# Retention with a mixture of attention experts: value products from the last key blocks, one write of v, a y table of one chunk, more buffers and a new order of the work

## The chip, the core and the metric

The kernel runs on one core of a Trainium2 chip. The core has a matrix engine (TensorE, PE in the profile; its weight loads are PEld), a vector engine (DVE), a scalar engine (ACT), GpSimd (POOL), and a queue engine (SP) that issues nearly all transfers here. Each takes its instructions in a fixed order. Matrix products land in PSUM, eight banks of 512 float32 columns on 128 partitions. The metric is the time of one execution in microseconds (us).

## The reference

Two stages follow each other. The first is retention: for 4 batches and 8 heads a 64x64 state runs over 768 positions.

```python
for t in range(S):
    state = gamma[None, :, None, None] * state + np.einsum('bhd,bhe->bhde', k[:, :, t], v[:, :, t])
    y[:, :, t] = scale * np.einsum('bhd,bhde->bhe', q[:, :, t], state)
```

Its output, laid side by side for the heads, is the x (4 x 768 x 512) of the second stage: four attention experts with one head of 64 each, of which every position uses the two with the highest gate logits.

```python
logits = x @ w_gate                      # top 2 of 4 experts, softmax weights w over the two
for e in range(E):
    q = x @ wq[e]; k = x @ wk[e]; v = x @ wv[e]
    scores = scale * (q @ k.transpose(0, 2, 1))
    scores = np.where(causal, -1000000000.0, scores)
    a = softmax(scores)
    out += (weight of e where it was chosen) * (a @ v @ wo[e])
```

Everything is float32.

## The kernel before, in words

The sequence is cut into 24 chunks g of 128 positions (six to a batch) and into 8 units j of 384 positions (two to a batch, so the odd unit of a batch attends to twice as many keys as the even one).

**Retention.** A chunk's q and k come in one load (`qkT_t`, three buffers), its k and v in natural order in another (`kv_t`, two buffers); `kdecay` scales the latter with powers of gamma. `h1(m)`, for half a chunk, adds to the state in PSUM (`ps_st`) and forms the part of y that comes from the state so far (`sblk`); `h2` forms the products inside the chunk, for which the scores are masked into one buffer (`am`). Then the DVE scales y out of PSUM by a table (`ys`, L307; the table `yt` holds 768 positions and is loaded in six pieces of 256 KB), ACT makes its rounded half `xh` (L309) and POOL the remainder `xl` (L311). All matrix products of the second stage are made of such halves.

**Experts.** `vgate(j, i)` forms v and the gate logits of a chunk, `proj` the q and k of two experts at a time. v stands with positions on partitions, and the value products need it with 32 keys on partitions: so v (in `vt`, a buffer of the four `pr`) goes to DRAM (`vd`) and comes back from there in four pieces (`vx`). It is written by two transfers, one for two experts each:

```python
def keep():
    for c in range(2):
        dma(vd.t[c].rearrange("i q n -> q i n"), vt.t[:, c * CH * 128:(c + 1) * CH * 128])
```

`pair(j, m)`, for 64 query positions and all four experts: scores into two banks (one or two spans of at most 512 keys), minimum on the DVE (L553, L558; scores have the sign turned), exponential with its sum on ACT (L565, into `pr`), the factor of sum and gate weight (L584 to L592), the scaling on POOL (L598) and a transposition in 32x32 blocks on the DVE (L605, into `pta` or `ptb`). There are six pairs to a unit, m = 0 to 5, with 64 more keys each. `av(j, k0, k1)` multiplies blocks of 32 keys with v and adds them up in four banks; an even unit has 12 key blocks, an odd one 24, in groups of six. The first matmul of a bank's sum starts it afresh (`start=k == 0`), and since all columns have to be started there, the groups run from the first key block on, which needs all six pairs. Then ACT and DVE take the two halves of the result (`oh` L650, `ol` L655, two buffers each), `wout(j, i)` multiplies with wo, ACT copies the result into `ot` (two buffers, shared with y) and SP stores it.

**The order.** The functions record operations; what is emitted is the list of numbers ORDER, one order over all engines, and SLOTS says which buffer each operation takes. In it the stages of three units overlap. An engine's instructions stand in the order of that list and wait for what they read and for their buffers to come free. At the start stand twelve products of a zeroed tile (`warm`) that write nothing of use.

## Time and profile before

| what | us |
|---|---|
| three runs | 323.5, 325.57, 328.87; median 325.57 |
| the profiled execution | 326.64 |
| its span, from the first to the last instruction | 324.7 |
| PE busy in it | 293.5 |
| DVE, ACT, POOL busy | 182.6, 152.2, 155.0 |

An engine is counted as busy while one of its instructions runs. A row of the timeline gives the start and duration of a run of equal instructions, and in brackets how long the engine had been idle and who ended that. In the chain of waits each piece is either work or a transfer that the next piece waited for. [...]

### The profile page before, as it was taken

To read this page: it belongs to the slowest core of one execution; us is meant where nothing else is said; L and a number is where in the kernel's file an instruction comes from. 1 tells how busy PE (TensorE), PEld (TensorE's weight loads), DVE (VectorE), ACT (ScalarE), POOL (GpSimd) and SP (SyncE) were. 2 spreads that over 40 slices of the span, in tenths; PEclk is the share of its full clock that TensorE was granted. 3 is DMA by queue.
4 is the path that set the end of the run, shared out by engine and by line. 5 is a ranking of instruction groups with operands and counts; after the bars stand their busy time and mean duration, and the time that the engine had idled before them with its cause. 6 is when DMAs were issued, how large, how long until landed. Compare 5 with 4: busy or idle time off the path is not lost.

```text
span 324.7 us, 14996 instructions
## 1 busy us (share of the span) xinstructions
PE 293.5 (90%) x6530; PEld 237.9 (73%) x6530; DVE 182.6 (56%) x567; ACT 152.2 (47%) x495; POOL 155.0 (48%) x281
## 2 busy tenths in 40 slices
PE   3879999979889999798999999999869999899695
PEld 1569979957579877676888987687668987527484
DVE  0242346586855676564676665667347544698601
ACT  2225355454454564445474452756426344366302
POOL 0257463855576362453729437166093623347300
PEclk9979999999979999999999999999989999999999
DMA  7898755752583345438447603343740013403103
GB/s 224 291 353 277 274 155 173 237 129 91 149 173 99 121 129 161 144 98 211 133 159 231 167 15 114 88 158 117 225 115 4 2 45 98 135 0 126 65 6 129
DMA packets 17106, 45.64 MB, mean 141 GB/s; under 512 B 2576, under 2 KB 5392, under 8 KB 17040
## 3 DMA queue, kind: packets, MB, share of 16 engines
q1 hardware_dynamic: 16896, 44.55, 44.2%
q8 instruction: 51, 0.84, 1.1%
q10 hardware_dynamic: 144, 0.13, 0.1%
q14 instruction: 15, 0.12, 0.1%
HBM read 35.23 MB, written 9.44 MB: 138 GB/s over the span
## 4 chain that ended last, share of the span: by engine, by line
PE 66%; DMA 10%; DVE 7%; POOL 6%; issue 5%; ACT 3%; SPq 1%; POOLq 0%; ACTq 0%; DVEq 0%
PE ps L130 61%; PE ps_st L130 5%; POOL pr L598 4%; DMA vd<-pr 4%; DMA out_dram<-ot 3%; ACT pr L565 2%; DVE ptb L605 2%; DVE ps L558 1%; DMA kv_t<-in_kv_dram 1%; ACT ot L686 1%; DMA kdec_t<-in_kdec_dram 1%; DMA vx<-vd 1%; SPq L133 1%; POOL kv_t L232 1%; DVE pta L605 1%
## 5 line engine op out<-in xcount | busy, mean ns | idle before, releaser
L598 POOL TENSOR_SCALAR pr<-pr,fs,wq 128x512 f32<-128x512 f32 (+7 forms) x128 | 77.0, 610 | 45.8 <-DVE fs L587 32.2
L565 ACT ACTIVATE pr<-ps,mn 128x512 f32<-128x512 f32 (+7 forms) x128 | 66.2, 521 | 58.8 <-DVE mn L558 25.1
L130 PE MATMUL ps<-kt,qt 64*64 64x512 f32 (+7 forms) x512 | 49.7, 439 | 0.6 <-ACT pr L565 0.4
L130 PE MATMUL ps<-xh,qk_hi 128*128 128x384 f32 x128 | 45.3, 354 | 2.6 <-ACT pr L565 2.6
L130 PE MATMUL ps<-xh,qk_lo 128*128 128x384 f32 x128 | 43.6, 340 | 2.5 <-issue 2.5
L605 DVE STREAM_TRANSPOSE ptb<-pr 128x448 f32<-128x448 f32 (+5 forms) x48 | 38.0, 800 | 11.4 <-POOL pr L598 11.4
L130 PE MATMUL ps<-xl,qk_hi 128*128 128x384 f32 x128 | 43.5, 340 | 0.0
L130 PE MATMUL ps_st<-kv_t 64*64 64x64 f32 x704 | 31.1, 226 | 9.9 <-DVE kv_t L232 5.4
L130 PEld LDWEIGHTS ps_st<-kv_t 64*64 64x64 f32 x704 | 27.4, 139 | 16.7 <-issue 5.9
L558 DVE CUSTOM_DVE_ANT_0 ps<-ps,mask 128x64 f32<-128x64 f32 (+7 forms) x64 | 28.1, 463 | 16.9 <-PE ps L130 16.6
L311 POOL TENSOR_TENSOR xl<-ot,xh 128x512 fp32r<-128x512 f32 x24 | 30.9, 1285 | 11.8 <-ACT xh L309 11.0
L130 PEld LDWEIGHTS ps<-ptb,vx 32*64 32x64 f32 x1504 | 27.4, 130 | 11.8 <-issue 8.4
L130 PE MATMUL ps<-ptb,vx 32*64 32x192 f32 (+5 forms) x1504 | 31.7, 296 | 4.5 <-issue 2.7
L232 POOL TENSOR_TENSOR kv_t<-kv_t,kdec_t 128x512 f32<-128x512 f32 x23 | 24.3, 1060 | 15.8 <-DMA kv_t<-in_kv_dram 12.1
L130 PEld LDWEIGHTS ps<-xh,qk_hi 128*128 128x128 f32 x128 | 24.2, 189 | 10.1 <-ACT pr L565 4.3
L130 PE MATMUL ps<-qkT_t 64*64 64x64 f32 x768 | 29.1, 223 | 2.1 <-ACT mn L575 1.4
L291 ACT ACTIVATE sblk<-ps_st 128x256 f32<-128x256 f32 x44 | 16.9, 383 | 29.9 <-PE ps_st L130 23.7
L130 PE MATMUL ps<-qkT_t,sblk 64*64 64x64 f32 x704 | 30.2, 223 | 0.6 <-issue 0.6
L130 PE MATMUL ps<-am,kv_t 64*64 64x64 f32 x768 | 28.7, 223 | 1.0 <-DVE am L354 0.7
L130 PE MATMUL ps<-vg_hi,xh 128*128 128x260 f32 x96 | 29.0, 302 | 0.6 <-ACT pr L565 0.6
L130 PEld LDWEIGHTS ps<-qkT_t 64*64 64x64 f32 x768 | 26.5, 138 | 4.0 <-ACT mn L575 1.6
L130 PEld LDWEIGHTS ps<-am,kv_t 64*64 64x64 f32 x768 | 26.0, 138 | 2.3 <-issue 1.5
(77 smaller groups left out, 595.7 us busy)
## 6 DMA issues: line engine op xcount, KB each, us to landing
kv_t<-in_kv_dram SPq DMA_DIRECT2D x24, 512.0 KB
qkT_t<-in_qkT_dram SPq DMA_DIRECT2D x24, 512.0 KB
vx<-vd SPq DMA_DIRECT2D x32, 192.0 KB
out_dram<-ot SPq DMA_DIRECT2D x23, 256.0 KB
vd<-pr SPq DMA_DIRECT2D x16, 192.0 KB
yt<-in_ytab_dram SPq DMA_DIRECT2D x6, 256.0 KB
ptb<-in_wqk_dram SPq DMA_DIRECT2D x2, 256.0 KB
pr<-in_wqk_dram SPq DMA_DIRECT2D x2, 256.0 KB
```

What stands on the lines that cost most here:

```text
L130: done["last"] = nc.tensor.matmul(*args, **kw)
L133: done["dma"] = nc.sync.dma_start(*args)
L232: e.tensor_tensor(kk, kk, K["kdec"][:, 2 * c:2 * c + n, :, None].to_broadcast([128, n, HP, D]), op=OP.mult)
L291: lambda: nc.scalar.activation(sb, ST[b].t[:, :HP * D].rearrange("p (h d) -> p h d", h=HP), AF.Copy),
L311: lambda: nc.gpsimd.tensor_tensor(xl.t[:, :, sl], raw(), xh.t[:, :, sl], op=OP.subtract),
L558: lambda n=n, bk=bk, at=at: nc.vector.tensor_tensor_reduce(bk.t[:, :n], bk.t[:, :n], mask[:, BANK - n:], 1.0, mn.t[:, at - 2:at - 1] if tw ...
L565: lambda u=u, lo=lo, hi=hi, n=n, bk=bk, at=at: nc.scalar.activation(pr[u].t[:, lo:hi], bk.t[:, :n], AF.Exp, bias=mn.t[:, at:at + 1], scale ...
L598: lambda u=u, lo=lo, hi=hi, i=i: nc.gpsimd.tensor_scalar(pr[u].t[:, lo:hi], pr[u].t[:, lo:hi], fs.t[:, 2 + u:3 + u] if i + 1 < len(spans) ...
L605: lambda u=u: nc.vector.transpose(pt[u].t[:, :wide // T, m], pr[u].t[:, :wide].rearrange("p (b k) -> p b k", k=T)),
L686: nc.scalar.activation(ot.t, wb.t, AF.Copy)
```

## The change

- **Value products.** Eight matmuls of a zeroed part of `mask` (read as bfloat16) clear the four banks of a unit (`start=True`), and every product adds to them. The groups of six key blocks then run from the last to the first, and a group waits only for the pairs that have keys in it: the last group of a unit for the pairs 3 to 5, all groups before it for all six. The pairs are recorded from m = 5 down to 0.
- **v.** One transfer writes `vt` to DRAM, a row of 3,072 bytes to a partition; the four reads take pieces of 1,536 bytes instead of 6,144.
- **y.** A table of 128 positions (256 KB, loaded once) and a factor for each chunk and head pair take the place of the table of 768. Four instructions scale y, with 128 columns each, where there was one with 512.
- **Buffers.** `am` two instead of one, `oh` and `ol` four instead of two, `ot` three instead of two.
- **Start.** The memset of `mask` is cut in two, and `warm` needs the first 64 columns of it alone; `h2` of the first chunk and the first `h1` stand behind `warm`.
- **Order.** ORDER and SLOTS are new throughout.

```diff
-    AM = tag("am", 1, [128, 2, HP, SC])
+    AM = tag("am", 2, [128, 2, HP, SC])
...
-    OH = tag("oh", 2, [128, HS], F32R)
-    OL = tag("ol", 2, [128, HS], F32R)
-    OT = tag("ot", 2, [128, Dm])
+    OH = tag("oh", 4, [128, HS], F32R)
+    OL = tag("ol", 4, [128, HS], F32R)
+    OT = tag("ot", 3, [128, Dm])
...
-        op("DVE", "ys", 512, lambda: nc.vector.tensor_tensor(raw(), yy(), YT[:, g % NC], op=OP.mult),
-           r=[(y,), ("yt", g % NC)], w=[(ys,)], new=[ys])
+        def scaled():
+            for h in range(HP):
+                nc.vector.scalar_tensor_tensor(raw()[:, h], yy()[:, h], K["yf"][:, g % NC, h:h + 1], K["yt"][:, h],
+                                               op0=OP.mult, op1=OP.mult)
+
+        op("DVE", "ys", 512, scaled, r=[(y,), ("yt_t",), ("yf_t",)], w=[(ys,)], new=[ys])
...
-        def keep():
-            for c in range(2):
-                dma(vd.t[c].rearrange("i q n -> q i n"), vt.t[:, c * CH * 128:(c + 1) * CH * 128])
-
-        op("SP", "vd", 393216, keep, r=[(vt, x) for x in range(CH)], w=[(vd,)], new=[vd])
+        op("SP", "vd", 393216, lambda: dma(vd.t.rearrange("p c n -> p (c n)"), vt.t), r=[(vt, x) for x in range(CH)],
+           w=[(vd,)], new=[vd])
...
-                dma(vx.t[g * T:g * T + T].rearrange("p b n -> p (b n)"), vd.t[g // 2].rearrange("i q n -> i (q n)"))
+                dma(vx.t[g * T:g * T + T].rearrange("p (q a) n -> p q (a n)", q=4),
+                    vd.t[:, g // 2].rearrange("(q i) n -> i q n", i=T))
...
+        def first(k, h):
+            return max(0, (k - half * NB - h + 1) // 2)
+
         def fn():
+            if k1 == nk:
+                for u in range(NP):
+                    for h in range(2):
+                        for x in range(2):
+                            g = 2 * (x ^ u) + h
+                            zero = mask[g * T:g * T + T, :BANK - SC].bitcast(BF)
+                            mm(ab[u][h].t[rows(x), :NM * T], zero[:, :Hd], zero[:, :NM * T], start=True, stop=False,
+                               skip_group_check=True)
...
-                               start=k == 0, stop=k == nk - 1 - (1 - h), skip_group_check=True)
+                               start=False, stop=k0 == 0 and k == k1 - 1, skip_group_check=True)
...
-        return [(0.7, lambda m=m: pair(j, m)) for m in range(NM)]
+        return [(0.7, lambda m=m: pair(j, m)) for m in reversed(range(NM))]
...
-        u = [(2.0, lambda i=i: av(j, i * 6, i * 6 + 6)) for i in range(n)]
+        u = [(2.0, lambda i=i: av(j, i * 6, i * 6 + 6)) for i in reversed(range(n))]
```

What the new list moves is shown at two places. The first is the start of SP's queue, which holds the loads; `kv_t` and `qkT_t` are a chunk's inputs (512 KB each), `in_wvg`, `in_wqk` the weights (130 and 256 KB), `yt` the table of y. Before:

```order
L133 DMA kv_t_66<-in_kv_dram 128x1024
L133 DMA kdec_t<-in_kdec_dram 128x48
L133 DMA ot_109<-in_wvg_dram 128x260
L133 DMA ptb_103<-in_wqk_dram 128x512
L133 DMA ot_110<-in_wvg_dram 128x260
L133 DMA qkT_t_63<-in_qkT_dram 128x1024
L133 DMA qkT_t_64<-in_qkT_dram 128x1024
L133 DMA am_t<-in_amask_dram 128x64
L133 DMA pr_97<-in_wvg_dram 128x260
L133 DMA yt<-in_ytab_dram 128x512
L133 DMA kv_t_67<-in_kv_dram 128x1024
L133 DMA pr_98<-in_wvg_dram 128x260
```

The same place in the changed kernel:

```order
L134 DMA kv_t_66<-in_kv_dram 128x1024
L134 DMA kdec_t<-in_kdec_dram 128x48
L134 DMA qkT_t_63<-in_qkT_dram 128x1024
L134 DMA am_t<-in_amask_dram 128x64
L134 DMA qkT_t_64<-in_qkT_dram 128x1024
L134 DMA kv_t_67<-in_kv_dram 128x1024
L134 DMA qkT_t_65<-in_qkT_dram 128x1024
L134 DMA yf_t<-in_yfac_dram 128x24
L134 DMA ot_114<-in_wvg_dram 128x260
L134 DMA yt_t<-in_ytab_dram 128x512
L134 DMA kv_t_66<-in_kv_dram 128x1024
L134 DMA pr_98<-in_wvg_dram 128x260
```

The inputs of the first three chunks now stand ahead of the weights; the table of y is one load, where five more of its size followed. The load of `kv_t_66` for the third chunk is the second use of that buffer in both.

The second place is PE's end, on unit 7, the last. Before, the last score (`kt`, `qt`: pair 4, its second span) is followed by two output products (`wo`), and then by all value products of the unit, from the first key block on:

```order
L130 MATMUL ps_121<-kt_80,qt_76 64x192 x2
L130 MATMUL ps_117<-kt_79,qt_75 64x192 x2
L130 MATMUL ps_119<-wo_hi,oh_106 128x512
L130 MATMUL ps_119<-wo_lo,oh_106 128x512
L130 MATMUL ps_119<-wo_hi,ol_107 128x512
L130 MATMUL ps_119<-wo_hi,oh_105 128x512
L130 MATMUL ps_119<-wo_lo,oh_105 128x512
L130 MATMUL ps_119<-wo_hi,ol_108 128x512
L130 MATMUL ps_122<-wo_hi,oh_106 128x512
```

In the changed kernel the last score is pair 0, a single span; behind it stand the value products of unit 6, an output product, and the last group of key blocks of unit 7. These rows are that group's end, an output product of unit 6, and the start of the next group, the first that needs pair 0:

```order
L131 MATMUL ps_126<-ptb_105,vx_83 64x32 x2
L131 MATMUL ps_127<-ptb_104,vx_83 64x32 x2
L131 MATMUL ps_122<-wo_hi,oh_109 128x512
L131 MATMUL ps_122<-wo_lo,oh_109 128x512
L131 MATMUL ps_122<-wo_hi,ol_113 128x512
L131 MATMUL ps_122<-wo_hi,oh_108 128x512
L131 MATMUL ps_122<-wo_lo,oh_108 128x512
L131 MATMUL ps_122<-wo_hi,ol_112 128x512
L131 MATMUL ps_123<-ptb_105,vx_83 64x192 x2
L131 MATMUL ps_126<-ptb_105,vx_83 64x192 x2
```

Between PE's first score of unit 7 and the group that needs all its pairs there stood, before, the rest of unit 5's value products, five output products and the value products of unit 6; now it is seven output products, the value products of unit 6 and the last group of unit 7. Of the two output products of unit 6 that are left, one stands between the later groups of unit 7 and one behind the last of them, ahead of those that need its result.

## Rows read from the trace of the kernel before

**Rows 1.** The page: busy time and share of the span for each engine, and the span in 40 slices (tenths).
```profile
PE 293.5 (90%) x6530; PEld 237.9 (73%) x6530; DVE 182.6 (56%) x567; ACT 152.2 (47%) x495; POOL 155.0 (48%) x281
PE   3879999979889999798999999999869999899695
```

**Rows 2.** Busy time by stretch, the start: the stretch and its length, then for each engine busy time and instructions, the granted clock, the DMA share, GB/s.
```profile
2.00:10.00 8.00, 4.62 (x26) 2.33 (x27) 0.69 (x1) 1.34 (x4) 0.00 (x0) 1.00 0.97 314
10.00:20.00 10.00, 6.47 (x291) 5.43 (x292) 4.04 (x7) 2.71 (x7) 3.80 (x4) 0.99 0.85 314
20.00:23.30 3.30, 3.29 (x109) 3.02 (x103) 0.69 (x1) 1.01 (x2) 1.58 (x3) 0.52 0.98 297
```

**Rows 3.** The timeline of the start, of POOL, SP and PE: start, duration, instruction. The POOL rows are `kdecay` of the second and third chunk, the SP row the load of the third, the PE row the first product of `vgate`.
```profile
12.65 1.04 POOL L232 TENSOR_TENSOR kv_t<-kv_t,kdec_t 128x512 f32<-128x512 f32 x1 [11.39 <-DMA kv_t<-in_kv_dram]
14.22 0.33 SPq L133 DMA_DIRECT2D kv_t<-in_kv_dram  x1
17.94 1.42 POOL L232 TENSOR_TENSOR kv_t<-kv_t,kdec_t 128x512 f32<-128x512 f32 x1 [3.55 <-DVE am L354]
23.24 0.39 PE L130 MATMUL ps<-vg_hi,xh 128*128 128x260 f32 x1
```

**Rows 4.** Busy time by stretch, three stretches in which the write of v ran, with columns as in rows 2.
```profile
39.50:44.30 4.80, 4.23 (x138) 3.54 (x136) 1.20 (x6) 2.36 (x9) 2.58 (x4) 1.00 0.28 92
111.00:115.00 4.00, 4.00 (x116) 3.45 (x115) 2.77 (x6) 2.68 (x9) 3.23 (x6) 1.00 0.27 89
194.00:198.00 4.00, 4.00 (x119) 2.98 (x125) 1.82 (x10) 1.56 (x6) 2.28 (x6) 1.00 0.27 92
```

**Rows 5.** The chain of waits, two stretches: start, duration, what.
```profile
82.86 6.57 DMA vd<-pr
89.53 0.79 ACT pr L565 x2
...
225.65 6.61 DMA vd<-pr
```

**Rows 6.** Busy time by stretch around these two writes, with columns as in rows 2.
```profile
84.00:91.00 7.00, 4.37 (x156) 3.10 (x149) 6.00 (x16) 2.82 (x12) 4.18 (x8) 1.00 0.83 226
91.00:96.00 5.00, 5.00 (x120) 4.47 (x124) 3.05 (x12) 2.53 (x8) 3.40 (x5) 0.66 0.85 174
231.00:238.50 7.50, 6.48 (x190) 5.29 (x189) 1.78 (x8) 3.40 (x13) 3.17 (x9) 0.77 0.98 274
```

**Rows 7.** Busy time by stretch, the other places at which PE stood still, with columns as in rows 2.
```profile
66.00:74.00 8.00, 5.77 (x156) 3.98 (x147) 5.67 (x19) 4.01 (x15) 3.81 (x9) 1.00 0.40 96
133.00:138.00 5.00, 3.25 (x192) 2.94 (x192) 1.81 (x6) 2.48 (x8) 2.42 (x3) 1.00 0.07 15
148.00:151.00 3.00, 1.61 (x37) 0.98 (x39) 1.95 (x9) 2.48 (x10) 1.39 (x5) 1.00 1.01 221
238.50:245.00 6.50, 3.95 (x61) 2.94 (x61) 2.82 (x9) 1.51 (x6) 5.53 (x10) 1.00 0.16 43
```

**Rows 8.** Busy time by stretch, the end: from the first score of unit 7 to its last transposition, from there to the end of its value products, and the rest.
```profile
276.60:307.10 30.50, 25.93 (x499) 14.28 (x487) 24.21 (x70) 17.16 (x57) 16.00 (x37) 1.00 0.26 85
307.10:315.60 8.50, 8.42 (x355) 7.51 (x356) 0.00 (x0) 0.00 (x0) 0.00 (x0) 1.00 0.04 12
315.60:324.70 9.10, 4.91 (x65) 3.86 (x52) 1.58 (x5) 3.07 (x8) 0.00 (x0) 0.94 0.32 117
```

**Rows 9.** PE's timeline: a group of value products of unit 5, the two groups of unit 6, the first score of unit 7, the last score of unit 7, the first output product of unit 7 and the start of the next.
```profile
276.88 0.98 PE L130 MATMUL ps<-kt,qt 64*64 64x448 f32 x8
277.79 1.94 PE L130 MATMUL ps<-ptb,vx 32*64 32x192 f32 x96
295.21 1.96 PE L130 MATMUL ps<-pta,vx 32*64 32x192 f32 x96
298.12 1.49 PE L130 MATMUL ps<-pta,vx 32*64 32x96 f32 x88
299.53 0.85 PE L130 MATMUL ps<-kt,qt 64*64 64x192 f32 x8
316.52 0.50 PE L130 MATMUL ps<-wo_hi,oh 128*128 128x512 f32 x1 [0.44 <-ACT oh L650]
318.02 0.28 PE L130 MATMUL ps<-wo_hi,oh 128*128 128x256 f32 x1
```

**Rows 10.** Groups of DVE and ACT instructions by line and shape: line, engine, operation, names, shapes and count, then total and mean time (ns), then idle time before them and its releasers.
```profile
L307 DVE TENSOR_TENSOR ot<-ps,yt 128x512 f32<-128x512 f32 x24 | 16.4, 684 | 12.1 <-PE ps L130 4.1 <-DMA out_dram<-ot 3.4 <-DMA yt<-in_ytab_dram 3.1
L655 DVE TENSOR_TENSOR ol<-ps,oh 128x192 fp32r<-128x192 f32 x32 | 10.2, 349 | 22.8 <-ACT oh L650 22.6
L200 DVE TENSOR_TENSOR vg_lo<-pr,vg_hi 128x260 fp32r<-128x260 f32 x1 | 0.4, 430 | 0.9 <-ACT vg_hi L197 0.9
L197 ACT ACTIVATE vg_hi<-pr 128x260 fp32r<-128x260 f32 x2 | 0.8, 416 | 2.1 <-DMA pr<-in_wvg_dram 2.1
L492 DVE SCALAR_TENSOR_TENSOR gs<-gs 128x12 f32<-128x12 f32 x8 | 3.5, 434 | 0.4 <-ACT gs L506 0.2
```

**Rows 11.** The list of who waited for whom: engine and line, releaser, total, times, longest.
```profile
ACT pr L565 <- DMA vd<-pr: 8.1, 4, 3.5
PE ps L130 <- ACT pr L565: 5.7, 5, 2.6
PE ps L130 <- DVE am L354: 0.7, 1, 0.7
```

More of the change, by code (lines that the diff above doesn't have):

```diff
@@ L263, in h1 @@
         rr, ww, new = [], [], []
+        if m == 0:
+            rr.append(("warm",))
         if c:
@@ L328, in h2 @@
                 ww += [(XT[j][0], "n"), (XT[j][1], "n")]
+        if g is None:
+            rr.append(("warm",))
         if n is not None:
@@ L560, in pair @@
                            op0=OP.add, op1=OP.min, accum_out=mn.t[:, at:at + 1]),
-                       r=[(bk,), ("mask",), ("cmask_t",)] + [(mn, at - 2)] * two, w=[(mn, at), (bk,)], new=first)
+                       r=[(bk,), ("wu",), ("mask",), ("cmask_t",)] + [(mn, at - 2)] * two, w=[(mn, at), (bk,)], new=first)
             for u in range(2):
@@ L606, in pair @@
                    pt[u].t[:, :wide // T, m], pr[u].t[:, :wide].rearrange("p (b k) -> p b k", k=T)),
-               r=toks, w=[(pt[u], m)], new=[pt[u]] if m == 0 else [])
+               r=toks, w=[(pt[u], m)], new=[pt[u]] if m == NM - 1 else [])
     AB = {}
@@ L613, in av @@
         nk = NB * (half + 1)
-        if k0 == 0:
+        new = []
+        if k1 == nk:
             AB[j] = [[Buf(PB) for _ in range(2)] for _ in range(NP)]
+            new = [x for y in AB[j] for x in y]
         ab, pt = AB[j], PTB[j]
         vx = [VXB[j - 1 + i] for i in range(2)] if half else [VXB[j]]
+        def first(k, h):
+            return max(0, (k - half * NB - h + 1) // 2)
         def fn():
+            if k1 == nk:
+                for u in range(NP):
[5 more added lines that the diff above has]
+                               skip_group_check=True)
             for k in range(k0, k1):
-                own = k - half * NB
                 v, at = vx[k // NB].t, k % 4 * CH + k % NB // 4
@@ L624, in fn @@
                     for h in range(2):
-                        lo = max(0, (own - h + 1) // 2)
+                        lo = first(k, h)
                         if lo >= NM:
@@ L632, in fn @@
                                pt[u].t[g * T:g * T + T, k, lo:].rearrange("p m i -> p (m i)"),
-                               start=k == 0, stop=k == nk - 1 - (1 - h), skip_group_check=True)
+                               start=False, stop=k0 == 0 and k == k1 - 1, skip_group_check=True)
         op("PE", "av", (k0, k1, half), fn, r=[(vx[k // NB], g) for k in {k0, k1 - 1} for g in range(E)] +
-           [(pt[u], m) for u in range(2) for m in range(NM)], w=[(x,) for y in ab for x in y],
-           new=[x for y in ab for x in y] if k0 == 0 else [], mode="32x64")
-        if k1 < nk:
+           [(pt[u], m) for u in range(2) for m in range(min(first(k0, 0), first(k0, 1)), NM)] + [("wu",), ("mask",)],
+           w=[(x,) for y in ab for x in y], new=new, mode="32x64")
+        if k0:
             return
@@ L733, in head @@
     def head():
-        op("POOL", "ms", BANK, lambda: nc.gpsimd.memset(mask, 0.0), w=[("mask",)])
+        op("POOL", "ms", SC, lambda: nc.gpsimd.memset(mask[:, :SC], 0.0), w=[("wu",)])
+        op("POOL", "ms", BANK - SC, lambda: nc.gpsimd.memset(mask[:, SC:], 0.0), w=[("mask",)])
         wu = mask[:, :64].bitcast(BF)
@@ L752, in warm @@
                 mm(pbs[i % 6].t, wu, wu[:, None, :].to_broadcast([128, 4, 128]), start=True, stop=True)
-        op("PE", "warm", 0, warm, r=[("mask",)], w=[(pb,) for pb in pbs], new=pbs, mode="128x128")
+        op("PE", "warm", 0, warm, r=[("wu",)], w=[(pb,) for pb in pbs] + [("warm",)], new=pbs, mode="128x128")
         h2(None, 0)
@@ L883 @@
     "kt": "01230123",
[L884 removed]
+    "kv_t": "010101010101010110100100",
     "lg": "01010101",
[L886 to L889 removed]
+    "mn": "012100210210210210210210210210210210210210201201",
+    "oh": "0123012301012301",
+    "ol": "0123012301012301",
+    "ot": "01201201201201201201020102001201202020210210222012",
     "pr": (
[L891 to L892 removed]
+        "0123012303231032012301231032130312031202132031021310213203102130120213021320231203213010230232102013"
+        "021320130"
     ),
     "ps": (
[L895 to L897 removed]
+        "0123456012345613025430561345260124351062412435206413206435102651453604251360543162056314203546141643"
+        "5120435621035462531046201351460215604231540621354621306016325401254504635121251256041254032614521630"
+        "1523640152360413542615046153012462452364501501501235604315620431506215046302415634021465030236"
     ),
@@ L900 @@
     "pta": "0100100101",
-    "ptb": "0101010101",
-    "qkT_t": "012012012012012010102102",
+    "ptb": "0110010101",
+    "qkT_t": "012012012012102120210201",
     "qt": "0123012301230123",
-    "su": "012012012012012012010120120120120120210210210210",
+    "su": "012101201201201201201201201201201201201201201201",
     "vd": "01010101",
-    "vx": "01201201",
+    "vx": "01210121",
     "wq": "01010101",
```

40 lines of the change are left out of this document (13 added, 27 removed), and 134 rows, old and new, of the table ORDER.

## The prediction, made before the changed kernel ran

> **What bounds the kernel now.** I read the page first, then the busy times by stretch, then the chain of waits where PE stood still, and last the timelines of the two ends. PE is busy for 293.5 of 324.7 us, and no other engine for more than 56% [rows 1]. So a change pays where PE stands still or runs at half clock, and the reader is to look for these places in the slices: the first three and the last few, and weak digits between.
>
> The start is bound by transfers: the DMA share is 0.97 and 0.85, at 314 GB/s, and PE is busy 4.62 of 8 and 6.47 of 10 us [rows 2]. The second chunk's `kdecay` starts at 12.65 and the third's at 17.94, both after their loads, and only the product at 23.24 (`vgate`) opens the stretch in which PE is nearly always busy [rows 3].
>
> In the middle two writes of v stand in the chain with 6.57 and 6.61 us [rows 5]: the exponentials behind them need one of the four `pr` buffers, which v holds until it is written; ACT waited 8.1 us for that in all [rows 11]. Around them PE stands still for 7 - 4.37 = 2.63 and 7.5 - 6.48 = 1.02 us, and the granted clock falls to a mean of 0.66 over 5 us and 0.77 over 7.5, which costs 5 x 0.34 = 1.7 and 7.5 x 0.23 = 1.7 us [rows 6]. That is 7.0 us. Where a write runs with little else, the DMA share is 0.27 to 0.28 and the rate 89 to 92 GB/s [rows 4], against 314 at the start: about a quarter of the 16 engines is at work.
>
> Other stalls of PE lie at 66, 133, 148 and 238 us: 2.23 + 1.75 + 1.39 + 2.55 = 7.9 us [rows 7].
>
> At the end, unit 7's softmax paces PE. From its first score to its last transposition 30.5 us go by, of which PE works 25.93 and the DVE 24.21; then PE works without a pause for 8.5 us on value products, and in the last 9.1 us it is busy for 4.91 [rows 8].
>
> **The change, part by part.** The sum is made against the profiled execution, 326.64 us (the median of the runs, 325.57, is 1.1 lower).
>
> *Start.* The queue moves 314 GB/s from about 2 us on [rows 2]. Before, 3.08 MB are queued up to the second chunk's `kv_t`: 2 + 9.8 = 11.8 us, and POOL began at 12.65, so 0.8 more is to be added. Now it is 2.15 MB: 2 + 6.9 + 0.8 = 9.7, 3.0 us sooner. The third chunk's load needs the first buffer back, which `h1` of the first chunk gives up; that needs the second chunk's q and k (1.63 MB, 8.0 us) and 1.5 us of PE, so it can be issued at 9.5, while the queue still has work. With 3.61 MB it lands at 14.3, against a `kdecay` at 17.94: 3.6 sooner. The four pieces of `in_wvg` end at 4.53 MB, 17.2 us; the last two take two ACT and two DVE instructions of 0.42 and 0.43 us [rows 10], so `vgate` starts at about 18.9 instead of 23.24 [rows 3]. I take **-4.2**. It would be less, down to -2, if PE, idle between loads, stays at the half clock that it has from 20.0 to 23.3 (0.52) [rows 2]; it is hardly more than -5, which is what the saved 1.3 MB of table and the new sequence give together. The earlier `warm` costs nothing: it lies where PE waits for the first load.
>
> *The write of v.* The bytes are the same, 393 KB. No row shows the new form. Its bounds are the present rate, 90 GB/s (4.4 us), and the rate of the loads, 314 GB/s (1.3 us) [rows 2, 4]. I take a value near the second, since the new write has, like a load, one long row for each of 128 partitions. Then the two waits end some 3 us sooner, and with them go the 7.0 us of stall and half clock: **-7**, between 0 and -7.
>
> [...]
>
> The reads of v now move pieces of 1,536 bytes. The old write moved such pieces at 90/4 = 22 GB/s an engine, the loads run at 314/16 = 20 [rows 2, 4], so I cost them at nothing.
>
> *The end.* I take the stretches of rows 8 again. First, from the first score of unit 7 to the group that needs all its pairs: PE has 3,648 score columns, at 0.91 us for 448 (276.88 to 277.79) 7.4 us; seven output products of 1.5 (316.52 to 318.02), 10.5; unit 6's groups with 1.9 and 1.4, and unit 7's last group like the second of these, 1.4 [rows 9]. That is 22.6. The DVE has the 24.21 of before without unit 5's four `ol` (4 x 0.35) [rows 10] and without some 1 us of unit 6's leftovers: 21.8, and it was busy for 79% of that stretch [rows 8]; at this pace 27.5. So the DVE sets it, at 27.5 instead of 30.5: -3.0. Second, the rest of unit 7's products, 8.5 - 1.5 - 1.4 = 5.6, and two output products, 3.0: 8.6 instead of 8.5. Third, the 0.9 us between 315.6 and 316.52 is covered by an output product that stands behind the last group. And PE has 1.2 us more to do inside these stretches (31.2 against 30.0), so the first score comes 1.2 sooner. Sum -3.0 + 0.1 - 0.9 - 1.2 = **-5.0**. If the DVE keeps the 30.5 it is -2; if PE alone sets it (22.6), -10.
>
> *Clearing the banks.* 8 units x 8 matmuls. A group of 96 value products with 192 columns takes 1.94 us, 20 ns each [rows 9]; 64 x 20 ns = **+1.3**. They are cheaper where they fall in a stall; each as long as an output product's matmul (1.5/6 = 0.25 us) they would be +16, which I keep for the upper end only.
>
> *y.* From 512 columns in 684 ns and 192 in 349 [rows 10] a column costs 1.05 ns, so 128 cost 282 and four 1.13 us, 0.44 more than one of 512. 24 times that is 10.7 us of DVE time on an engine that is 56% busy. Most hides behind PE; the wait before `ys` is PE's (4.1 of 12.1 us) or a transfer's, and the wait for the table (3.1) goes. I take **+0.7**, between 0 and +10.7.
>
> *Buffers.* PE's wait for `am` is 0.7 us [rows 11]: nothing. *The new order in the middle* moves everything; the 7.9 us of rows 7 may go or come twice. I take 0, with -8 and +8 as bounds.
>
> Sum: 326.6 - 4.2 - 7 - 5 + 1.3 + 0.7 = **312.4**.
>
> **The rivals.**
> 1. *More goes than that.* The groups of unit 7 and of the units before wait for fewer pairs, and the middle's stalls go as well (-8), with a DVE that has no gaps at the end (-3): 301. For it: each of those stalls is a wait for another unit's softmax or buffer. Against: a new order meets new waits.
> 2. *The gain is eaten.* The middle gains as many stalls again (+8), and the end keeps its 30.5 us (+3): 323. For it: the end is paced by the DVE, and y makes the DVE busier. Against: the start and the write of v do not hang on that.
> 3. *Slower: y becomes a bound.* If four `SCALAR_TENSOR_TENSOR` cost what the row of that operation with the highest mean shows, 434 ns [rows 10], y takes 1.74 us, 1.05 more a chunk, and since `xh`, `xl` and every projection follow, 24 x 1.05 = 25 us could lie on the path: 337. It is slower than now by over 2% once 19 of the 24 chunks pay that in full. Against: that row has 12 columns, so its mean holds waits; and y is seldom last now.
> 4. *The write stays at a quarter of the engines:* 319.
>
> **How the numbers follow.** A measurement here tells a difference of about 2% (6.5 us) from none, so faster means under 319.1, slower over 332.1. Chances: the forecast (306 to 319) 0.50, rival 1 0.18, rival 2 0.20, rival 3 0.07, rival 4 0.05. The predicted time is 312. From 303 to 322 lie the forecast's cases, rival 4, two thirds of rival 1 and about half of rival 2: 8 in 10. Faster: 0.50 + 0.18 and half of rival 4, with a little of rival 2, 0.72; slower: rival 3, 0.07; the same: 0.21.
>
> **What would show it.** `kdecay` of the third chunk near 14.3 and `vgate` near 19 us; writes of v of under 2 us and no wait of ACT for them; the stretch from unit 7's first score to its last transposition at 25 to 28 us; four `ys` of some 0.28 us each; clearing matmuls of some 20 ns. The forecast is wrong if PE's stalls in the middle exceed 12 us, or if `ys` stands in the chain of waits with more than a few us.

## The result, and the profile after

The changed kernel takes **301.86 us** (median of 4 runs, 298.50 to 302.38), against 324.76 for the kernel before on the same chip: a ratio of 0.9285, 95% interval [0.9191, 0.9379]. The forecast was 312 with a range of 303 to 322, so the time lies just below the range; the forecast's sum had a gain of 14.2 us (326.6 - 312.4), and 22.9 came. The profiled execution has a span of 299.5 us (run time 301.34), 25.2 less than the one before.

The page of the changed kernel: busy time, PE and the granted clock (PEclk, the share of its full speed that TensorE was given) in 40 slices [rows 1], the new scaling of y [rows 10], and the write of v with the median time from issue to landing.

```profile
PE 282.0 (94%) x6594; PEld 234.3 (78%) x6594; DVE 192.6 (64%) x639; ACT 152.5 (51%) x495; POOL 154.6 (52%) x282
PE   7669999967999999999999999998999999999994
PEclk9969999999999999999999999999999999999999
L308 DVE SCALAR_TENSOR_TENSOR ot<-ps,yf_t,yt_t 128x128 f32<-128x128 f32 x96 | 26.6, 341 | 8.0 <-PE ps L131 7.7
vd<-pr SPq DMA_DIRECT2D x8, 384.0 KB, 2.7
```

PE's slices are full from the fourth on, except for the ninth (6) and the tenth (7), at 60 to 75 us, one 8 and the last; the clock stays at full speed, 1.00, from 23.8 us to the end. The DVE has 10.0 us more to do; y alone takes 26.6 - 16.4 = 10.2 more.

Who waited for whom, in the changed kernel [rows 11]: engine and line, releaser, total, times, longest. "issue" is a wait for which the profile shows no releaser.

```profile
ACT pr L568 <- DMA vd<-pr: 2.2, 3, 0.8
PE ps L131 <- ACT pr L568: 0.4, 1, 0.4
PE ps L131 <- issue: 3.9, 5, 1.8
PE ps_st L131 <- issue: 1.4, 2, 0.9
```

ACT's wait for the write fell from 8.1 to 2.2 us, PE's wait for the exponentials from 5.7 to 0.4. Of PE's waits the largest sum, 3.9 + 1.4 = 5.3 us, is now one for which the profile names no releaser.

The start of the changed kernel: the third chunk's `kdecay`, the first product with the value weights [rows 3], the load that stands in the chain, and busy time by stretch [rows 2].

```profile
14.07 1.04 POOL L232 TENSOR_TENSOR kv_t<-kv_t,kdec_t 128x512 f32<-128x512 f32 x1 [1.17 <-PE ps L131]
21.13 0.58 PE L131 MATMUL ps<-vg_hi,xh 128*128 128x260 f32 x1
11.99 6.33 DMA qkT_t<-in_qkT_dram
15.90:18.30 2.40, 0.00 (x0) 0.00 (x0) 0.47 (x2) 0.46 (x2) 1.27 (x1) 0.72 0.89 252
18.30:23.80 5.50, 5.44 (x108) 5.32 (x109) 2.62 (x7) 2.73 (x6) 2.85 (x3) 0.50 1.03 398
```

The end, in the three stretches of [rows 8]:

```profile
258.30:281.50 23.20, 22.80 (x415) 14.40 (x415) 21.92 (x62) 15.50 (x53) 15.14 (x34) 1.00 0.27 82
281.50:290.30 8.80, 8.80 (x299) 7.50 (x299) 0.52 (x2) 2.57 (x7) 0.00 (x0) 1.00 0.34 123
290.30:299.50 9.20, 4.84 (x27) 4.00 (x25) 1.05 (x4) 2.29 (x5) 0.00 (x0) 1.00 0.32 116
```

So the start (to the first `vgate`) took 21.1 instead of 23.2 us, the end (from unit 7's first score) 41.2 instead of 47.8, and the middle 237.2 instead of 253.6: 16.4 of the 25.2 us of the span lie in the middle, where the forecast's own terms gave 5. In two further executions of the same kernel (experiments 7 and 8) the first `vgate` came at 20.7 and 20.3 us.

### The profile page after: what moved, and what is told of

It reads as the page before. It is cut to its first block, busy times and chain, and to the rows that moved or that the text cites. A ratio compares the mean times of both kernels' runs of the same rounds, so it can differ in the third digit from the quotient of the medians.

```text
span 299.5 us, 15148 instructions
## 1 busy us (share of the span) xinstructions
PE 282.0 (94%) x6594; PEld 234.3 (78%) x6594; DVE 192.6 (64%) x639; ACT 152.5 (51%) x495; POOL 154.6 (52%) x282
## 4 chain that ended last, share of the span: by engine, by line
PE 85%; DMA 8%; issue 2%; SPq 1%; ACT 1%; DVE 1%
PE ps L131 81%; DMA qkT_t<-in_qkT_dram 7%; PE ps_st L131 5%; DMA vd<-pr 2%; SPq L134 1%; ACT pr L568 0%; DVE ot L308 0%; ACT qt L415 0%; ACT ot L701 0%; DVE pr L699 0%; ACT pr L447 0%; ACT lg L444 0%; ACT mn L578 0%
## 5 line engine op out<-in xcount | busy, mean ns | idle before, releaser
L131 PE MATMUL ps<-kt,qt 64*64 64x512 f32 (+7 forms) x512 | 44.9, 435 | 0.6 <-ACT qt L415 0.6
L608 DVE STREAM_TRANSPOSE ptb<-pr 128x768 f32<-128x768 f32 (+5 forms) x48 | 37.6, 799 | 7.3 <-POOL pr L601 7.2
L561 DVE CUSTOM_DVE_ANT_0 ps<-ps,mask 128x384 f32<-128x384 f32 (+7 forms) x64 | 28.2, 468 | 12.2 <-PE ps L131 11.7
L131 PEld LDWEIGHTS ps_st<-kv_t 64*64 64x64 f32 x704 | 26.4, 137 | 9.1 <-issue 5.0
L131 PE MATMUL ps_st<-kv_t 64*64 64x64 f32 x704 | 30.0, 222 | 3.3 <-POOL kv_t L232 1.9
L131 PE MATMUL ps<-qkT_t 64*64 64x64 f32 x768 | 28.3, 223 | 3.8 <-DMA qkT_t<-in_qkT_dram 3.8
L308 DVE SCALAR_TENSOR_TENSOR ot<-ps,yf_t,yt_t 128x128 f32<-128x128 f32 x96 | 26.6, 341 | 8.0 <-PE ps L131 7.7
L131 PE MATMUL ps<-ptb,vx 32*64 32x192 f32 (+5 forms) x1504 | 29.7, 295 | 0.0
L131 PEld LDWEIGHTS ps<-qkT_t,sblk 64*64 64x64 f32 x704 | 26.0, 137 | 3.3 <-issue 3.0
L131 PE MATMUL ps<-am,kv_t 64*64 64x64 f32 x768 | 27.8, 223 | 0.7 <-issue 0.7
```

The source lines that it names most:

```text
L131: done["last"] = nc.tensor.matmul(*args, **kw)
L308: nc.vector.scalar_tensor_tensor(raw()[:, h], yy()[:, h], K["yf"][:, g % NC, h:h + 1], K["yt"][:, h], op0=OP.mult, op1=OP.mult)
L561: lambda n=n, bk=bk, at=at: nc.vector.tensor_tensor_reduce(bk.t[:, :n], bk.t[:, :n], mask[:, BANK - n:], 1.0, mn.t[:, at - 2:at - 1] if tw ...
L608: lambda u=u: nc.vector.transpose(pt[u].t[:, :wide // T, m], pr[u].t[:, :wide].rearrange("p (b k) -> p b k", k=T)),
```

## The experiments

**How the traces are split.** For each operation of PE (a projection, a score, a group of value products) I take the time from its first product to the next operation's, less the quarter-fastest time of its kind in the kernels before and after. What is left over in the middle is split in three. *Code*: pauses of over 0.5 us that end 1.1 to 1.75 us after a piece of PE's own program has landed, at a place where the program passes from one piece to the next (experiment 4 tells how that was read). *Half clock*: half of the time with a granted clock of 0.50, an estimate of what it cost. *Other*: the rest, above all waits for another engine or a load. Each row is one profiled execution, and its time is the ratio of all its runs to the kernel before. Two further executions of the changed kernel have about 1 and 2 us more of code than its row here, so differences of under 2 us in this table show nothing.

```
                                ratio    start  middle  end  | over in the middle: code  half  other
before                          1        23.2   253.6   47.8 |  32.0                8.8   3.4   19.7
before, one write (b1)          1.010    23.5   256.0   49.1 |  34.3               13.4   8.5   12.4
before, fewer loads (b4)        0.979    23.8   244.8   48.4 |  23.1                2.8   0.7   19.5
before, both (b2)               0.962    22.7   242.3   49.4 |  20.6                6.2   1.7   12.7
after                           0.9285   21.1   237.2   41.2 |  16.8                6.4   1.3    9.1
after, two writes (x1)          0.970    21.9   250.6   40.7 |  30.2                4.9   5.1   20.3
after, first blocks first (x4)  0.949    21.2   246.6   41.7 |  26.2               11.5   6.5    8.2
after, 64 places on (x6)        0.953    20.5   247.1   42.5 |  26.8               11.2   7.5    8.0
after, fewer loads (x7)         0.896    20.6   232.4   41.2 |  12.0                1.0   1.5    9.5
after, burst spread (x12)       0.914    20.7   236.2   40.8 |  15.9                5.4   0.3   10.2
```

**1. The write alone, and the write undone.** In the kernel before, and the reverse in the changed one:

```diff
-            for c in range(2):
-                dma(vd.t[c].rearrange("i q n -> q i n"), vt.t[:, c * CH * 128:(c + 1) * CH * 128])
+            dma(vd.t.rearrange("p c n -> p (c n)"), vt.t)
```

> The kernel before with one edit: v is written in one transfer of 128 rows, and read back from that layout; list and buffers are as before. Theory 'sum' (the forecast's term, -7): 318 us, the two waits of 6.6 us in the chain at about 3, and ACT waiting under 2 us for them in place of 8.1. Theory 'write is all' (the middle's 16 us come from the write alone): 308 to 311. Theory 'order' (the write hides as soon as the list gives room, and the list is what pays): 320 to 324, since the list of before puts other waits behind the same places. Writes near 1.3 us each by the first two, and near 5 if the new form runs on a quarter of the engines.

Measured: 329.61 us, ratio 1.010 [1.004, 1.016]. No theory held on the time. Yet most of what was foreseen of the write came: 2.7 us from issue to landing (1.3 was forecast, near 5 at a quarter of the engines), no wait of ACT for it left, and "other" falls by 19.7 - 12.4 = 7.3 us. New pauses of PE and half clock ate it (+4.6 and +5.1). Two pieces of the chain of waits of this run, the stretch around the second, and PE's wait without a releaser, first of the kernel before and then of this run:

```profile
43.85 2.76 issue
```

```profile
95.01 2.12 issue
```

```profile
91.50:94.60 3.10, 3.10 (x121) 2.85 (x123) 3.10 (x8) 0.85 (x3) 3.08 (x4) 1.00 1.08 279
94.60:97.10 2.50, 0.41 (x28) 0.24 (x15) 1.21 (x10) 1.33 (x5) 1.30 (x3) 1.00 0.83 239
98.60:102.00 3.40, 3.40 (x23) 2.96 (x25) 1.20 (x3) 0.16 (x1) 3.06 (x7) 0.50 0.00 0
```

```profile
PE ps L130 <- issue: 6.9, 7, 2.5
PE ps_st L130 <- issue: 1.9, 2, 1.6
```

```profile
PE ps L130 <- issue: 14.7, 8, 3.6
```

PE stands still for 2.1 us in the midst of a group of value products, just after a stretch with a DMA share of 1.08, and soon afterwards runs at half clock for 3.4 us.

> The changed kernel with one edit: v written in two transfers in the old layout again; all else stays. 'Sum': 302 + 7 = 309, with ACT waiting some 8 us for the buffers that v holds. 'Write is all': 314 or more. 'Order': 302 to 305, because this list puts other work where a write is under way.

Measured: 316.10 us, ratio 0.970 [0.964, 0.976], 14 us over the changed kernel. That is the number of "write is all", but not for its reason alone: "other" rises by 20.3 - 9.1 = 11.2 us, the half clock by 3.8. ACT again waits for the write:

```profile
ACT pr L570 <- DMA vd<-pr: 10.1, 3, 5.0
```

So the old write costs 7 us of waits in the old order and 11 in the new one.

**2. All of the change but its order.** The changed kernel with the list of before (`ORDER` and `SLOTS` of before, without the table's loads and with the warm products first), pairs and value products from the first key block on.

> The change without its order: one write of v, clearing, y from a factor and a table of one chunk, four half buffers, two am, three ot, but the list of before (the table's loads leave it, the warm products stand first), with the pairs and the value products from the first key block on as before. 'Sum' (the order gives the end's 5 us, and nothing in the middle): 302 + 5 = 307. 'Order' (the list gives the end and most of the middle too, some 10 us): 313 to 318, PE's excess over its dense times in the middle near 25 us in place of 17. 'Write is all': 305 to 308, like 'sum', but then the first run of this set is near 310.

Measured: 327.65 us, ratio 0.995 [0.990, 1.001]. The rest of the change gains next to nothing without the order, which is more than any theory had for it: with the other parts in place the order, together with the value products from the last key block on, takes off 1 - 0.9285/0.995 = 6.7%, 22 us.

**3. The value products from the first key block on,** in the new order:

```diff
-        u = [(2.0, lambda i=i: av(j, i * 6, i * 6 + 6)) for i in reversed(range(n))]
+        u = [(2.0, lambda i=i: av(j, i * 6, i * 6 + 6)) for i in range(n)]
```

> The changed kernel with the value products of each unit from the first key block on, as before the change. A first group needs all pairs of its unit then, so in units 1, 5 and 7, where it stood ahead of the last transposition, it is put right behind it; all other places stay, and so does the clearing. The forecast's term for the end had 1.4 to 1.9 us of value products inside the stretch that the softmax paces: +2 to +5, so 304 to 307, all of it in the last 45 us. Theory 'the list is what pays, not this freedom': 301 to 303.

Measured: 312.14 us, ratio 0.949 [0.941, 0.957]. Longer than expected, and elsewhere: the end takes 41.7 us against 41.2, so the freedom to begin a unit with its last blocks is worth 0.5 us there, in this list. The loss is in the middle, +5.1 of pauses and +5.2 of half clock, while "other" does not grow. The groups that were moved also shift places in PE's program, which by itself can cost as much (experiment 4), so this is the price of one list and not of the direction.

**4. What the pauses are.** The trace has 51 packets of a queue of its own (`q8 instruction`), 0.84 MB, so 16 KB each; PE has 6,594 products, so one piece for every 6,594/51 = 129 of them with their weight loads. That the pieces hold PE's program is my reading of this match and of what follows. In all kernels of the table, each idle time of PE of over 0.5 us in the middle that has no releaser in the profile ends at a product with the number 93 + 127.5 k, within 5, counted from 0, and no idle time of over 0.5 us with a releaser does: 860, 1496, 2771, 4427, 5064 in the kernel before, 1242, 1370, 1497, 4814 in the changed one. A piece takes some 1 us to move (1.08 and 1.07, the medians in the kernels before and after), and PE goes on 1.1 to 1.75 us after it has landed. Moving the program by 64 places tests this:

```diff
-            for i in range(12):
+            for i in range(8):
                 mm(pbs[i % 6].t, wu, wu[:, None, :].to_broadcast([128, 4, 128]), start=True, stop=True)
+            for i in range(68):
+                mm(pbs[i % 6].t[:, :32], wu, wu[:, :32], start=True, stop=True)
```

> The changed kernel with the warm products cut differently: 8 of 512 columns and 68 of 32 in place of 12 of 512, in the same wait for the first load. Everything else stays, so all later products of PE stand 64 places further along its program. Theory 'code': PE's pauses that end some 1.2 to 1.7 us after a 16 KB piece of code has landed (six after the start, 6.5 us in all) lie where the program passes from one piece to the next, every 127 or 128 products; they move to other products, 64 places away, and since the list was not made for this the time is 302 to 312. Theory 'buffers and loads': the pauses stay at the same products and the time stays at 301 to 303.

Measured: 313.11 us, ratio 0.953 [0.948, 0.958]: 2.6% lost by moving places alone. The pause inside `h1` of step 15 (62.7 us, 1.99) is gone, a new one of 3.4 us stands in unit 0's last group of value products, one of 2.9 in the first `vgate`, others follow later; all numbers fit the same row (478, 1498, 3792, 4176, 4942). Theory "code" holds. The piece of the chain, and the stretches around it:

```profile
70.72 3.12 issue
```

```profile
68.00:70.60 2.60, 2.60 (x170) 2.47 (x166) 2.30 (x7) 1.38 (x4) 2.19 (x6) 1.00 0.92 272
70.60:73.90 3.30, 0.18 (x14) 0.07 (x9) 1.18 (x2) 0.55 (x2) 2.18 (x3) 0.88 0.32 126
73.90:80.00 6.10, 6.10 (x139) 4.41 (x143) 3.41 (x10) 2.81 (x12) 0.37 (x3) 0.51 0.01 3
```

In seven traces of the table (before, b1, b2, after, x6, x7, x12) a piece begins to move a median 0.6 to 0.8 us after PE has passed into the piece before it where the DMA share of the next microsecond is under 0.1, and 1.5 to 2.4 us after it where that share is over 0.7. With 1 us to move and 1.1 to 1.75 us until PE goes on, that is an estimated 3 us without other transfers, and 127 short products (20 ns each in a group of value products [rows 9]) are over in 2.6 us.

**5. Why a piece comes late.** From the fourth chunk on, only q and v are loaded, in the kernel before, with one write, and in the changed kernel:

```diff
-dma(qb.t, qkT[b, c])
+dma(qb.t[:, :2 - (g > 2)], qkT[b, c, :, :2 - (g > 2)])
-dma(nb.t, kv[b, c])
+dma(nb.t[:, g > 2:], kv[b, c, :, g > 2:])
```

> The kernel before with v written in one transfer, and from the fourth chunk on only q and v are loaded; k stays that of an earlier chunk in the same buffer (part of the input is left out, the instructions of the engines are the same). 11 of 45 MB of transfers go. Theory 'code behind data': the 16.7 us in which PE stands still for its own code come from pieces that queue behind data; they fall under 9, with the half clock after them, and the time is 310 to 318. Theory 'code, but the products are simply too short': the pauses stay at 14 to 19 us and the time at 326 to 331.

> The changed kernel with only q and v loaded from the fourth chunk on, as in the run beside it (k is that of an earlier chunk). 'Code behind data': 6.5 us of such pauses are left to save, and PE's wait for a late chunk (2.7 us at 15.6 us): 294 to 299, a smaller gain than the kernel before with one write has. 'Products too short': 299 to 302.

> The kernel before with only q and v loaded from the fourth chunk on (k stays that of an earlier chunk), and v still written in two transfers: the control for the run that had both. Theory 'the write is worth its 7 us, and late code hid it' : 321 to 325, so that the single write, which came to 0.962 of the kernel before with these loads, takes 6 to 9 us off once the code comes in time. Theory 'the write is worth nothing in the old order': 314 to 318, the same as with the single write; then the fewer loads alone made that gain.

Measured: b2 316.04 us, 0.962 [0.957, 0.968]; x7 294.65, 0.896 [0.891, 0.901]; b4 319.11, 0.979 [0.973, 0.986]. With fewer loads the pauses in the middle fall from 13.4 to 6.2 (b1 to b2), from 6.4 to 1.0 (after to x7) and from 8.8 to 2.8 us (before to b4), though PE's program and the length of its products are the same: what the theory 'code behind data' foresaw, without showing what holds a piece back. And with fewer pauses in the way, the single write alone (b4 to b2) takes off 1.7%, some 5.5 us: a little under the 6 to 9 of its theory, and b4's time lies between the ranges of the two theories. PE's wait without a releaser in x7:

```profile
PE ps L131 <- issue: 1.1, 2, 0.8
PE ps_st L131 <- issue: 0.8, 1, 0.8
```

> The change without its order (the old list), and from the fourth chunk on only q and v loaded. It had 16.9 us of pauses for code and 13.7 us of half clock with all loads, and took 1.00 of the kernel before. Theory 'the order pays by letting code come in time': both nearly go, and the ratio comes to 0.93 or less, within 3.5% of the changed kernel with these loads (0.896); what is left between them is the end's 8 us. Theory 'the order pays by other waits too': 0.945 to 0.965, as the kernel before with the single write has (0.962), and over 6 us more in the middle than the changed kernel with these loads, with little code in it.

Measured: 318.23 us, 0.973 [0.964, 0.981]. Only 2.3% less than with all loads (0.995), and 8.6% over the changed kernel with these loads: a miss for the theory that late code is all, and above the range of the other one. Its profiled execution was 4 us longer than its median, so I do not split it. But late code has not gone from it. PE's wait without a releaser, and the stretch before the longest of these pauses:

```profile
PE ps L131 <- issue: 13.0, 10, 4.6
```

```profile
226.00:228.80 2.80, 2.78 (x165) 2.54 (x164) 1.84 (x9) 0.12 (x2) 2.17 (x7) 1.00 0.87 236
```

SP issues two loads of a chunk's k and v, one of a chunk's q and k, and four reads of v within 5 us just ahead of it, and the piece that PE lacks moves at 231.0 us, 4.3 us after PE has passed into the one before. So fewer loads do not mend every list: this one still has its burst.

**6. Scaling y by one instruction:**

```diff
-            for h in range(HP):
-                nc.vector.scalar_tensor_tensor(raw()[:, h], yy()[:, h], K["yf"][:, g % NC, h:h + 1], K["yt"][:, h],
-                                               op0=OP.mult, op1=OP.mult)
+            nc.vector.tensor_tensor(raw(), yy(), K["yt"], op=OP.mult)
```

> The changed kernel with y of a chunk scaled by one instruction of 512 columns in place of four of 128; the factor of the chunk is left out, so the output is scaled differently from the second chunk of a batch on. 24 x (1.11 - 0.68) = 10 us of DVE time go. By the forecast's term (+0.7 of 10.7 on the path): 301. If the DVE sets the last units (94% busy in the stretch of unit 7's softmax): 297 to 300. Lower than 297 only if y stands on PE's path in the middle.

Measured: 302.00 us, 0.919 [0.914, 0.924]; the changed kernel came to 0.9247 and 0.9254 in its two further timings. By these ratios y costs 2 to 3 us, but the intervals overlap, so it is between nothing and some 3 us. The theories were stated in microseconds of another chip (the kernel before took 328.49 us here), and the run does not decide between them: in the stretch of unit 7's softmax the DVE is as busy as in the changed kernel (21.86 against 21.92 us), since no y falls into it.

**7. The start.** Three pieces of `in_wvg` ahead of the third chunk's k and v on SP, the fourth chunk's q and k right behind it; then the same with two products of 512 columns in PE's waits:

```diff
-L134 DMA kv_t_66<-in_kv_dram 128x1024
 L134 DMA pr_98<-in_wvg_dram 128x260
-L134 DMA qkT_t_63<-in_qkT_dram 128x1024
 L134 DMA pr_99<-in_wvg_dram 128x260
 L134 DMA ot_116<-in_wvg_dram 128x260
+L134 DMA kv_t_66<-in_kv_dram 128x1024
+L134 DMA qkT_t_63<-in_qkT_dram 128x1024
...
+            for _ in range({3: 1, 4: 1}.get(m, 0)):
+                mm(PB.tiles[6][:64], z, z[:, None, :].to_broadcast([128, 8, 64]), start=True, stop=True)
```

> The changed kernel as it is, timed beside the three others of this set so that they can be compared with it on one chip. All theories: 0.92 to 0.94 of the kernel before.

> The changed kernel with four rows of SP's queue moved in the start: the other three pieces of the first weights go ahead of the third chunk's k and v, which blocks the queue until its buffer is free at 10.5 us, and the fourth chunk's q and k directly behind it. PE's wait for that chunk (15.9 to 18.4 us) should shrink to under 1 us, the stretch at half clock with it, and the first product with the value weights come at 17.5 to 18.5 instead of 21.1. By this 2.5 to 3.5 us less, a ratio of 0.917 to 0.922 against the kernel before if the changed one has 0.9285. Rival: the transfers share one rate, so what comes sooner makes the next piece late (the third chunk's v, or the weights of q and k), and less than 1 us is won.

> The same, with one load of the ninth chunk moved ahead of two reads of v as well, and two products of 512 columns put into PE's waits at 14 and 16 us (on a bank that the next user clears, so nothing of the result changes), so that the clock finds PE at work. If the half clock of 6.8 us in the start goes: 1 to 2 us less than with the queue alone. Rival: the two products shift all later places of PE's program by two, and the pauses for code move; then anything from -2 to +4 us.

Measured beside the changed kernel (302.73, 0.9247): 302.64 us, 0.927 [0.920, 0.935], and 303.44, 0.933 [0.926, 0.939]. A miss for the first: `vgate` began at 20.6. PE's wait for the load fell to 0.3 us, but a pause without a releaser of 2.2 us stood at 12.3 us; the unedited kernel's execution beside it has the same two, 0.3 and 1.7 us, so the wait that was to go is not there in every execution. In the second it began at 19.3, and the mean granted clock of its profiled execution was 0.994, against 0.989 in the unedited kernel's beside it; but the two products (four rows in the trace) moved all later places, and one pause of 2.9 us came in at 204 us: its rival.

**8. Spreading a burst,** with all places kept. In the changed kernel, six reads of v and three loads run together from 50 to 61 us, and no piece of code moves from 51.3 to 62.2 us. DMA packets of that stretch, of the next one, and the chain there:

```profile
q1 hardware_dynamic: 1263, 2.66, 90.5%
```

```profile
q1 hardware_dynamic: 24, 0.04, 7.7%
q8 instruction: 1, 0.02, 5.2%
```

```profile
61.41 1.16 PE ps L131 x64
...
62.91 1.77 issue
```

PE passes into the piece before it at 59.0 us; the piece that it needs at 62.7 us begins to move only at 62.3, when the burst is over. SP's rows were moved so:

```diff
 L134 DMA kv_t_67<-in_kv_dram 128x1024
+L134 DMA vx_82<-vd_120 32x4x384 x4
+L134 DMA qkT_t_65<-in_qkT_dram 128x1024
 L134 DMA vd_121<-pr_98 128x768
 L134 DMA kv_t_66<-in_kv_dram 128x1024
-L134 DMA vx_82<-vd_120 32x4x384 x2
...
```

> The changed kernel as it is, once more, as the measure for the three beside it on the same chip: 0.92 to 0.94 of the kernel before.

> The changed kernel with five rows of SP's queue moved: the four reads of unit 0's v and the load of the ninth chunk's q and k go ahead of the write of unit 1's v, so that they run at 42 to 48 us, where the DMA share is 0.08 to 0.66, and not in the burst of 50 to 61 us. PE's program is the same. Theory 'code behind data': the pauses at 62.7, 67.6 and 72.1 us (4.2 us together) shrink to under 1.5, and 0.6 us of wait for q and k go: 3 us less than the run beside it, a ratio lower by 0.008 to 0.012. Theory 'products too short': the pauses stay, the ratio is the same within 0.003.

> The same, with the start of the queue reordered and two products put into PE's waits at 14 and 16 us as in an earlier run, where the first product with the value weights came 1.8 us sooner but all later places of the program moved; here the warm products are cut (four of 512 columns and two of 512 in float32) so that every later place is where it was. 1.5 to 2 us less than the run beside it with the spread burst, a ratio near 0.910 to 0.915. If the sooner start only moves other waits: no gain over that run.

Measured beside the changed kernel (302.25 us, 0.925 [0.919, 0.932]): **298.38 us, 0.914 [0.909, 0.919]**, and 298.94, 0.916 [0.910, 0.921]. The first holds on the time: the ratio is 0.011 lower, and no run of it (297.35 to 299.49) is as long as any of the changed kernel beside it (299.76 to 303.14). Stretches of the changed kernel, then of this one:

```profile
42.00:48.00 6.00, 6.00 (x92) 5.55 (x88) 4.67 (x18) 3.74 (x15) 3.02 (x5) 1.00 0.32 91
50.00:62.00 12.00, 11.57 (x151) 10.09 (x147) 8.91 (x40) 7.36 (x24) 5.82 (x13) 1.00 0.88 230
62.00:66.00 4.00, 2.23 (x83) 1.28 (x76) 1.93 (x9) 2.04 (x9) 2.45 (x6) 1.00 0.08 23
```

```profile
42.00:48.00 6.00, 6.00 (x126) 5.86 (x130) 4.59 (x21) 4.24 (x17) 3.20 (x6) 1.00 0.96 245
50.00:60.00 10.00, 10.00 (x104) 9.04 (x104) 7.12 (x35) 6.34 (x21) 5.13 (x11) 1.00 0.49 148
60.00:66.00 6.00, 5.47 (x283) 4.33 (x279) 5.33 (x19) 4.07 (x13) 3.93 (x10) 1.00 0.44 120
```

The pause at 62.7 us is gone, PE's idle time from 60 to 66 is 0.53 us; one of 2.0 us remains at 68.6, so not all three shrank, and one of 1.8 us stands at 196.7. In the table the pauses of the middle fall by 1.0 us alone, and the two profiled executions of this set lie 1.7 us apart, not 3.9: the traces account for a part of the gain. The time is lower than that of both kernels. The sooner start of the other version gained nothing on top: in that execution `vgate` came at 22.0 us.

## Why the prediction was wrong

The direction and most terms were right; the range missed by 1 us. By its steps:

- **The new order in the middle, "I take 0": this is the step that failed.** With the other edits in place the order and the direction of the value products are worth 22 us (experiment 2), some 8 of them in the end (49.1 in b1 against 41.2). In the middle, the old order with one write (b1) has 13.4 + 8.5 = 21.9 us of pauses for code and half clock, the new one 6.4 + 1.3 = 7.7; the "other" waits differ by 3.3 only. Counted from the kernel before, the split reads otherwise: of 15.2 us less over in the middle, 10.6 are other waits (7.3 of them the write's), 2.4 pauses and 2.1 half clock, since the single write brings in pauses that the new order takes out again. Either way some 11 us came in the middle beyond the 5 that were forecast. The working read the stalls of rows 7 as waits for another unit's softmax or buffer (rival 1 says so). Three of them, 1.61 + 1.75 + 2.55 = 5.9 of the 7.9 us, at 71, 135 and 240 us, were pauses for code. The chain of the kernel before has them:

```profile
71.25 1.61 issue
...
134.83 1.76 issue
...
240.06 2.55 issue
```

  The DMA share around the second, 0.07 [rows 7], should have ruled out a transfer, and an "issue" in the chain a buffer; nothing else in the text asked what PE waited for. The window count also missed what hides under "busy": the split finds 32.0 us over in the middle, where rows 6 and 7 gave 7.0 + 7.9.
- **The write of v, -7:** right as a price of waits, 7.3 us in the old order. Wrong as a sum: alone it gained nothing, because the time that it frees went into pauses for code and half clock.
- **The start, -4.2:** -2.1, near its lower bound. `kdecay` came at 14.07 (14.3 forecast), but the fourth chunk's q and k landed 6.33 us after issue, PE stood from 15.9 to 18.3 us and then ran at half clock (0.50 from 18.3 to 23.8 us); the text had named that clock as the way to -2. In the two further executions this wait is 0.3 and 1.4 us, with 1.7 and 0.7 us of pauses for code beside it, and `vgate` came at 20.7 and 20.3: the start stayed short of its term in each.
- **The end, -5:** -6.6, or -7.8 with the 1.2 us of PE's work that by the working's estimate moved in. The first stretch took 23.2 us, not 27.5: the DVE is busy for 94% of it, not for 79%, and PE's own 22.6 was right (22.80). That the DVE sets it fits experiment 3, where PE has 0.9 us less to do there and the stretch stays as long (below); its pace was mis-sized. Beginning with the last key blocks is not the reason (experiment 3: 0.5 us).
- **Clearing, +1.3:** the 64 products are busy for 3.0 us, by the group's row, 47 ns each and not 20; nothing larger shows. **y, +0.7:** 1.11 us a chunk (1.13 forecast), and experiment 6 bounds its cost by some 3 us.
- **The range** held rival 1 (301 us) to two thirds only. That rival has the number, with -8 for the middle and -3 for the end, at a chance of 0.18; its reason for the end came, but that for the middle, waits for fewer pairs, is not what the traces show, so its number is in part luck.
- **The signs** that were named: writes of v of 2.7 us, not under 2; a last softmax stretch of 23.2 us, not 25 to 28; `kdecay` as forecast. PE's idle time in the middle was to be over 12 us if the forecast was wrong; it fell from 13.4 to 6.1 us, and the forecast was wrong on the other side.

The group of clearing products, and the last softmax stretch in experiment 3:

```profile
L131 PE MATMUL ps<-mask 32*64 32x192 bf16 x64 | 3.0, 264 | 0.6 <-ACT pr L568 0.4 <-DVE ot L308 0.2
```

```profile
267.79:290.85 23.06, 21.84 (x330) 13.52 (x330) 21.95 (x62) 15.70 (x54) 15.18 (x34) 1.00 0.26 82
```

Open: how much of the time that the old order keeps with fewer loads (x11) is late code, and how the 22 us of the order split between waits that the traces name and pauses, for one list against another, beyond these single executions. When PE asks for the next piece was read from traces and not tried by itself.

## What to carry to other kernels

Where an engine in a full row of work stands still and the profile names no releaser, look at the packets of its own program: here pieces of 16 KB, one for some 128 products, which began to move 0.6 to 0.8 us after PE had passed into the piece before where little else moved, and 1.5 to 2.4 us after it where much did (medians, experiment 4). That short products add to it is an estimate from their 20 ns each. Moving transfers out of one burst took off 1.2% here (experiment 8). An order written out by hand is made for one set of durations: parts of a change tried alone in the old order can gain nothing (1.010, 0.995) though together with a new order they give 7%. And an edit that adds products to PE's program moves all later places in it, so compare versions that keep the places.

## What was not expected of the hardware

64 places in PE's program are worth 2.6% (experiment 4). A pause can cost more than itself: in b1, 1.5 us after the end of one of 2.12 us, the granted clock was 0.50 for 3.4 us (98.6 to 102.0), and in x6, after one of 3.12 us, it was 0.51 for 6.1 us (73.9 to 80.0). With half of that time added, an estimate, these pauses cost 3.8 and 6.2 us, about twice their own length. Not each is followed by such a stretch: after the 2.55 us at 240 us in the kernel before, the granted clock was 1.00 up to 276 us.

The write of v ran as two transfers at a DMA share of 0.27 to 0.28 and 89 to 92 GB/s [rows 4]. As one, where no other data moved (112.4 to 113.6 us in the changed kernel), it ran at 0.83 and 328 GB/s, and landed 2.3 us after its issue; the median of the eight is 2.7, against 6.57 and 6.61 in the old chain [rows 5]. Why the form of the write makes this difference was not shown, and whether the code waits behind that write in particular was not tried.
